# A mixer kernel on one core: nine r tiles beside attention, another order of the weight loads, and transposes on TensorE in both batches

## The chip, the cores and the metric

One core of a Trainium2 chip runs the kernel. Its engines are TensorE (PE, with the weight loads as PEld), VectorE (DVE), ScalarE (ACT), GpSimd (POOL) and SyncE (SP), which issues all DMAs here. The metric is the device time of one execution in microseconds, the median over several runs.

## The reference

Three blocks in a row, in float32, for 2 batches of 448 tokens and 768 channels:

```python
scores = scale * q @ k.T                       # 12 heads of 64, causal mask
x = softmax(scores) @ v                        # heads side by side: (2, 448, 768)
h = np.maximum(xt @ w_tok1, 0.0) @ w_tok2      # token mix, 448 -> 256 -> 448
u = x + h.transpose(0, 2, 1)
h2 = np.maximum(u @ w_ch1, 0.0) @ w_ch2        # channel mix, 768 -> 1536 -> 768
y = u + h2
# then a gated block: gelu(y @ w_in), layer norm of one half, a spatial 448 x 448
# product, the gate, w_out, and y added again
```

Most weights arrive as 8-byte floats and are decoded on the chip.

## The kernel before, in words

**Attention** (lines 251 to 558) goes over 24 heads, `n` = 0 to 23, batch 0 first, in pairs of heads (`pair`, line 400). Each head has two halves. For each half `probabilities` (line 327) multiplies q and k on PE (`s_ps`, line 345), masks and takes the maximum on DVE (line 350, tiles pe and mx), and exponentiates on ACT (line 359). The probabilities must then be transposed (tile pT). There are two ways. By DMA: ACT casts to a 16-bit high part (line 371), POOL subtracts for the low part (line 372, tile hl), SP issues a transposing DMA (line 373). On PE, with `on_pe`: four transposing matmuls into PSUM (line 365, t_ps), one eviction on ACT (line 367) and one on DVE (line 368). Only half (1, 1) of a pair can go on PE. `values` (line 386) multiplies by v (x_ps). After four heads `token_mix` (line 438) makes two channel tiles of u (a_ps, u_ps, tiles uh and ul).

**The channel mix** has twelve r tiles of 128 columns. One r tile for one batch is 18 matmuls of 448 columns (`mm3`, lines 185 to 187, r_ps), and needs one tile of w_ch1, which `load_w` (line 143) loads as 768 columns of 8 bytes (wraw, two buffers), decodes (`decode`, lines 127 to 131, on ACT and DVE), copies to a high part (line 140) and subtracts for the low part on POOL (`sub`, line 101, wlo). Three buffers hold decoded tiles.

The first NF0 = 8 r tiles of batch 0 are computed beside attention: `up_third` (line 495) emits a third of a tile, six matmuls, after each head of batch 1 from its fourth on, two after each of the last three; the rest follows as whole tiles (`up`, line 512). After attention the loop of line 633 computes batch 1 of the first eight tiles and both batches of the other four, loading those eight a second time. In between it asks for w_ch2 (`load_w2`, line 606) and scales r to 16 bits (`split_r`, line 594). Then come y = r times w_ch2 (y_ps, lines 671 to 696) and the gated block.

**What sets the order.** Each engine runs a fixed list. A scheduler makes the lists from a simulated timeline: of the instructions that are ready it takes the one of highest priority, which is the place in the program, moved by `tc.high_priority(offset=...)`; a negative offset moves it back. `tc.issue_after(ins)` keeps the block's instructions on the engine of `ins` behind it. `marks[n]` is the last transposing DMA issued up to head n; before, r tile m's load stands behind marks[10 + m].

Of the kernel before, what the change touches and what calls it, by code (L numbers as in the profile page):

```python
# [28 lines left out]
def mixer_kernel(  # L29
# [28 lines left out]
    GH = 4  # L58
    NT = T // P
    WC = 768  # L60
    NF0 = 8
    AHEAD = 4
    VAHEAD = 2
    LATER = 1500

    def f32(ap):
        return ap.bitcast(F32)
# [72 lines left out]
            nc.scalar.copy(hi, m)  # L140
        sub(lo, m, hi)

    def load_w(src, pool=wpool, bufs=3):

        k = src.shape[1]
        hi = pool.tile([P, WC // P, P], F32R, tag="whi", name="whi", bufs=bufs)[:, :k, :]
        lo = pool.tile([P, WC // P, P], F32R, tag="wlo", name="wlo", bufs=bufs)[:, :k, :]
        load64(hi.rearrange("p a f -> p (a f)"), lo.rearrange("p a f -> p (a f)"), src.rearrange("p a f -> p (a f)"))
        return hi, lo

    def absmax(dst, src):
# [65 lines left out]

    r_of = {}

    def channel_up(m, batches, pool, psum):  # L220

        wh, wl = load_w(w_ch1[m])
        for b in batches:
            us = slice(b * S, (b + 1) * S)
            pr = psum.tile([P, 512], F32, tag="d", name="r_ps")
            mm3(pr[:, :S], [((wh[:, c, :], wl[:, c, :]), (u_hi[c][b], u_lo[c][b])) for c in range(NCC)])
            r_done(m, b, pr, pool)
# [23 lines left out]
    with ExitStack() as at:  # L251
# [75 lines left out]
        def probabilities(qp, k2, hd, half, on_pe):  # L327

            ps = ps_s.tile([P, NP], F32, tag="s", name="s_ps")
            if (hd, half) == (1, 0):
                pe, mx = pes[count[0] % len(pes)], mxs[count[0] % len(pes)]
            else:
                pe = xp.tile([P, NP], F32, tag="pe", name="pe", bufs=NPE)
                mx = stp.tile([P, 2], F32, tag="mx", name="mx")
            todo, o = [], 0
            for j, i in enumerate(HALVES[half]):
                w = KW[i]
                if i > 0 or hd == 0:  # L340
# [13 lines left out]
            bias = mx  # L354
            if not on_pe:
                bias = stp.tile([P, 2], F32, tag="bias", name="bias")
                nc.scalar.add(bias, mx, math.log(PSCALE))
            for j, i, cs in todo:
                nc.scalar.activation(pe[:, cs], pe[:, cs], AF.Exp, bias=bias[:, j:j + 1], scale=-1.0)  # L359
            pT = hlp.tile([P, 2, NP // P, P], F16, tag="pT", name="pT", bufs=4)  # L360
            if on_pe:
                tp = ps_e.tile([P, 512], F32, tag="d", name="t_ps")
                for c in range(NP // P):
                    cs = slice(c * P, (c + 1) * P)
                    nc.tensor.matmul(tp[:, cs], pe[:, cs], ident, is_transpose=True, start=True, stop=True)
# [7 lines left out]
            last[0] = nc.sync.dma_start_transpose(  # L373
                out=pT.rearrange("p a c q -> p (a c) q"), in_=hl.rearrange("p a n -> p (a n)")
            ).ins
            return pT


# [59 lines left out]
        def token_mix(b, g, xf, xh, xl):  # L438
            N = GH * D
            pa = ps_a.tile([P, NT, N], F32, tag="a", name="a_ps")  # L440
            for t in range(NT):
                ts = slice(t * P, (t + 1) * P)
                nc.tensor.matmul(pa[:, t, :], w1h[:, 0, ts], xh[:, 0, :], start=True, stop=False)
                nc.tensor.matmul(pa[:, t, :], w1l[:, 0, ts], xh[:, 0, :], start=False, stop=False)
                mm3(pa[:, t, :], [((w1h[:, c, ts], w1l[:, c, ts]), (xh[:, c, :], xl[:, c - 1, :])) for c in range(1, NQ)], True)
            ah = xp.tile([P, NT, N], F32R, tag="ah", name="ah")
            al = xp.tile([P, NT, N], F32R, tag="al", name="al")
            nc.scalar.activation(ah, pa, AF.Relu)
# [22 lines left out]
                nc.vector.tensor_sub(u_lo[cc][b], pu[:, :S], f32(u_hi[cc][b]))  # L471


        last, last_x, marks = [None], [None], []
        order = [(b, h) for b in range(B) for h in range(H)]
        qks, vss = {}, {}

# [6 lines left out]
        def prepare_v(n):  # L484
            if n < len(order) and n % 2 == 0:
                b, h = order[n]

                with tc.high_priority(offset=-80):
                    vr, _ = v_begun.pop(n, None) or load_v(b, h // 2)
                    vss[b, h // 2] = prep_v(b, h // 2, vr)  # L490

        dense = list(range(NF0))
        thirds = []

        def up_third():

            if not thirds:
                m = dense.pop(0)
                with tc.issue_after(marks[H - 2 + m]), tc.high_priority(offset=-LATER):
                    wh, wl = load_w(w_ch1[m])  # L500
# [3 lines left out]
            mm3(  # L504
                pr[:, :S],
                [((wh[:, c, :], wl[:, c, :]), (u_hi[c][0], u_lo[c][0])) for c in (c0, c0 + 1)],
                c0 > 0, not thirds,
            )
            if not thirds:
                r_done(m, 0, pr, rpool)  # L510

        def up():

            m = dense.pop(0)
            with tc.issue_after(marks[H - 2 + m]):
                channel_up(m, [0], rpool, ps_e)

        def decode_tok(c):
            with tc.issue_after(last_mx[0]), tc.high_priority(offset=-80):
# [11 lines left out]
        for n, (b, h) in enumerate(order):  # L531
            if n > 0:
                prepare(n + AHEAD)
                prepare_v(n + VAHEAD)
            if n == GH - 1:
                for c in range(2, NQ):
                    load_tok(c)
                for c in range(NT):
                    load_tok2(c)
            if h % GH == 0:  # L540
                x = (
                    xp.tile([P, GH // 2, 7, D], F32, tag="xf", name="xf", bufs=2),
# [1 line left out]
                    xp.tile([P, NQ - 1, GH * D], F32R, tag="xl", name="xl"),  # L544
                )
            if h % 2 == 0:
                it = pair(b, h // 2, h % GH // 2, qks[b, h // 2], x, b == 0 and h > 0)
            next(it, None)
            marks.append(last[0])
            if h % GH == GH - 1:  # L550
                token_mix(b, h // GH, *x)

            if b == 1 and h >= 3:
                for _ in range(1 if h < H - 3 else 2):
                    up_third()

        while dense:
            up()
# [351 lines left out]
```

## Time and profile before

| | us |
|---|---|
| median of 3 runs | 415.42 (412.61 to 415.44) |
| profiled execution, its own time | 416.44 |
| its span, first to last instruction | 414.7 |
| PE busy | 391.3 (94%) |
| DVE, ACT, POOL busy | 282.4, 250.4, 202.5 |
| mean granted clock of TensorE | 0.988 of full speed |

The profile is of one execution. Busy times are sums over an engine's instructions; matmuls are pipelined, so PE counts as busy while one is under way. The DMA share is the mean busy share of 16 DMA engines; some stretches read above 1. Attention and the first r tiles fill the span to 168.8 us, the packed r stage goes to 228.3, the y stage to about 315, the gated block to the end.

### The profile page before, as it was taken

What the parts mean: (1) busy time and instruction counts of PE and PEld (TensorE: products, weight loads), DVE (VectorE), ACT (ScalarE), POOL (GpSimd) and SP (SyncE); (2) the same over time, 40 slices, a digit from 0 to 9 for tenths busy, and PEclk for the clock granted to TensorE, in tenths of its full rate; (3) what the DMA queues carried; (4) which work ended last, traced back from release to release, by engine and by line L of the source; (5) the groups of instructions that cost most, each with busy time, mean ns of one, the idle gap of its engine ahead of it and who ended that gap; (6) DMA issues with size and microseconds to landing.
All of it is one profiled execution on the core that took longest, in us unless ns stands there. A gap on an engine that the chain in (4) does not pass through costs nothing.

```text
span 414.7 us, 7332 instructions
## 1 busy us (share of the span) xinstructions
PE 391.3 (94%) x2622; PEld 267.9 (65%) x2622; DVE 282.4 (68%) x696; ACT 250.4 (60%) x483; POOL 202.5 (49%) x208
## 2 busy tenths in 40 slices
PE   5879899799898998999999999999999999999996
PEld 3447778588787887999889555555544445554554
DVE  6887866887785426444446787557898996469742
ACT  3988767787876555565679886344256556553210
POOL 3759864997686466062261447145121348315300
PEclk9999999799999999999999999999999999999999
DMA  7999899979997544466643313534623131100122
GB/s 220 246 238 232 161 206 271 246 186 236 265 247 140 137 112 144 163 217 229 207 149 102 90 65 114 186 107 134 222 73 90 51 103 51 52 2 0 68 92 107
DMA packets 61747, 61.77 MB, mean 149 GB/s; under 512 B 47888, under 2 KB 53264, under 8 KB 61712
## 3 DMA queue, kind: packets, MB, share of 16 engines
q1 hardware_dynamic: 61712, 61.32, 55.6%
q8 instruction: 20, 0.33, 0.3%
q14 instruction: 15, 0.12, 0.1%
HBM read 47.29 MB, written 2.75 MB: 121 GB/s over the span
## 4 chain that ended last, share of the span: by engine, by line
PE 25%; DVE 18%; ACT 12%; POOL 10%; DMA 9%; issue 8%; SPq 0%; POOLq 0%; ACTq 0%
DMA wraw<-in 7%; PE r_ps L186 5%; PE r_ps L185 5%; PE r_ps L187 5%; ACT r L172 3%; POOL hl L372 3%; PE o_ps L187 2%; PE o_ps L185 2%; PE o_ps L186 2%; DVE y L173 2%; DVE wm L131 2%; DVE w2m L131 1%; ACT wm L127 1%; PE u_ps L459 1%; POOL w L179 1%
## 5 line engine op out<-in xcount | busy, mean ns | idle before, releaser
L345 PE MATMUL s_ps<-k,q 128*128 128x64 f32 (+3 forms) x216 | 57.2, 405 | 11.5 <-DVE mx L350 4.8
L372 POOL TENSOR_TENSOR hl<-pe,hl 128x512 f16<-128x512 f32 x43 | 52.3, 1223 | 25.6 <-ACT hl L371 24.5
L101 POOL TENSOR_TENSOR wlo<-wm,whi 128x768 fp32r<-128x768 f32 x20 | 39.9, 1994 | 40.4 <-ACT whi L140 40.2
L185 PE MATMUL r_ps<-uh,whi 128*128 128x448 f32 x144 | 55.1, 383 | 0.0
L130 DVE TENSOR_SCALAR wm<-wm 128x768 int32<-128x768 int32 (+2 forms) x35 | 22.9, 655 | 46.9 <-ACT wm L127 46.9
L186 PE MATMUL r_ps<-ul,whi 128*128 128x448 f32 x144 | 53.9, 374 | 0.0
L187 PE MATMUL r_ps<-uh,wlo 128*128 128x448 f32 x144 | 53.0, 368 | 0.0
L185 PE MATMUL y_ps<-r,w 128*128 128x448 f16 x144 | 50.8, 353 | 0.0
L127 ACT ACTIVATE wm<-wraw 128x768 f32<-128x768 f32 (+2 forms) x35 | 27.8, 798 | 38.0 <-DMA wraw<-in 24.1
L186 PE MATMUL y_ps<-r,w 128*128 128x448 f16 x144 | 50.7, 352 | 0.0
L187 PE MATMUL y_ps<-r,w 128*128 128x448 f16 x144 | 50.6, 352 | 0.0
L345 PEld LDWEIGHTS s_ps<-k,q 128*128 128x128 f32 x216 | 32.2, 207 | 22.5 <-DVE mx L350 6.7
L350 DVE CUSTOM_DVE_ANT_0 pe<-s_ps,mask 128x192 f32<-128x192 f32 (+3 forms) x84 | 34.6, 441 | 7.2 <-PE s_ps L345 6.4
L246 POOL TENSOR_TENSOR y<-yt,ul 128x448 f32<-128x448 f32 x12 | 15.8, 1319 | 46.4 <-DVE yt L244 46.4
L359 ACT ACTIVATE pe<-pe,bias 128x448 f32<-128x448 f32 (+3 forms) x74 | 35.6, 525 | 0.4
L131 DVE SCALAR_TENSOR_TENSOR wm<-wraw,wm 128x768 int32<-128x768 int32 (+2 forms) x35 | 32.8, 938 | 0.7
L396 PE MATMUL x_ps<-vh,pT 128*128 128x65 f16 (+1 forms) x240 | 26.9, 201 | 3.1 <-DMA pT<-hl 3.0
L371 ACT CAST hl<-pe 128x512 f16<-128x512 f32 x43 | 26.3, 611 | 5.9 <-DMA pT<-hl 4.7
L185 PEld LDWEIGHTS r_ps<-uh,whi 128*128 128x128 f32 x144 | 27.3, 190 | 3.0 <-issue 0.4
L186 PEld LDWEIGHTS r_ps<-ul,whi 128*128 128x128 f32 x144 | 27.2, 189 | 3.1 <-issue 0.6
L187 PEld LDWEIGHTS r_ps<-uh,wlo 128*128 128x128 f32 x144 | 27.2, 189 | 2.7 <-issue 0.2
L179 POOL TENSOR_TENSOR w<-w2m,w 128x768 f16<-128x768 f32 x12 | 21.2, 1787 | 15.8 <-ACT w L178 11.2
(212 smaller groups left out, 1016.0 us busy)
## 6 DMA issues: line engine op xcount, KB each, us to landing
wraw<-in SPq DMA_DIRECT2D x36, 768.0 KB, 4.5
wraw<-in SPq DMA_DIRECT2D x14, 512.0 KB, 3.8
vr<-in SPq DMA_DIRECT2D x12, 320.0 KB, 4.0
k<-in SPq DMA_DIRECT2D x12, 224.0 KB, 3.7
q<-in SPq DMA_DIRECT2D x24, 112.0 KB, 4.0
out<-ob SPq DMA_DIRECT2D x11, 224.0 KB, 1.9
wraw<-in SPq DMA_DIRECT2D x3, 256.0 KB, 4.6
pT<-hl SPq DMA_TRANSPOSE x43, 4.0
```

The lines of the kernel that those rows point to most:

```text
L101: nc.gpsimd.tensor_sub(lo, src, f32(hi))
L127: nc.scalar.activation(m, words.bitcast(F32)[:, :, 1], AF.Prelu, scale=2.0 ** -112, alpha=-(2.0 ** 32))
L131: nc.vector.scalar_tensor_tensor(mi, words[:, :, 0], 29, mi, ALU.logical_shift_right, ALU.bitwise_or)
L185: nc.tensor.matmul(ps, lh, rh, start=i == 0 and not begun, stop=False)
L186: nc.tensor.matmul(ps, lh, rl, start=False, stop=False)
L187: done.append(nc.tensor.matmul(ps, ll, rh, start=False, stop=ended and i == n - 1).ins)
L345: last_s[0] = nc.tensor.matmul(ps[:, o:o + m], qp[:, q0:q0 + P], k2[:, ks], start=True, stop=True).ins
L350: last_mx[0] = nc.vector.tensor_tensor_reduce(out=pe[:, cs], in0=ps[:, cs], in1=mask0 if i == 0 else mask[:, MASKS[i]], scale=-1.0 / math. ...
L359: nc.scalar.activation(pe[:, cs], pe[:, cs], AF.Exp, bias=bias[:, j:j + 1], scale=-1.0)
L371: nc.scalar.copy(hl[:, 0], pe)
L372: nc.gpsimd.tensor_sub(hl[:, 1], pe, hl[:, 0])
L396: nc.tensor.matmul(o, ph, vh[:, c, h, :D + 1], start=j == 0, stop=False)
```

## The change

- NF0 becomes 9. Thirds are placed by a table of heads, from head 11 on, and their matmuls get a priority 150 lower. Four tiles still follow whole.
- The load of r tile m stands behind the transposes of head BEHIND[m]; the loads get a priority of -800 instead of -1500; the low part is subtracted in three parts of 256 columns.
- The half (1, 1) is transposed on PE for pairs 1, 2, 3 and 5 of batch 0 and 1, 2 and 3 of batch 1 (before: 1 to 5 of batch 0).
- The token weights are asked for at heads 2 and 3 instead of both at 3, the second with a priority raised by 100; v is prepared with -40 instead of -80.
- With NF0 the loop after attention runs over tiles 0 to 4, 9 to 11 and 5 to 8.

```diff
-    NF0 = 8
+    NF0 = 9
-    LATER = 1500
+    LATER = 800
+    BEHIND = [10, 15, 13, 13, 17, 18, 19, 12, 15]
+    THIRDS = {11: 1, 14: 1, 15: 1, 17: 1, 18: 2, 19: 1, 20: 1, 21: 3, 22: 2, 23: 2}
+    ON_PE = [(0, 1), (0, 2), (0, 3), (0, 5), (1, 1), (1, 2), (1, 3)]
...
+    def load_parts(src, behind):
+        raw = wpool.tile([P, WC], mybir.dt.int64, tag="wraw", name="wraw", bufs=2)
+        w = WC // len(behind)
+        for i, ins in enumerate(behind):
+            cs = slice(i * w, (i + 1) * w)
+            with tc.issue_after(ins):
+                nc.sync.dma_start(raw[:, cs], src[:, cs])
+        return raw
...
+        if behind is None:
+            load64(hi1, lo1, src)
+        else:
+            m = wpool.tile([P, WC], F32, tag="wm", name="wm", bufs=3)
+            decode(m, src, raw=load_parts(src, behind))
+            nc.scalar.copy(hi1, m)
+            w = WC // 3
+            for i in range(3):
+                cs = slice(i * w, (i + 1) * w)
+                sub(lo1[:, cs], m[:, cs], hi1[:, cs])
...
-                with tc.high_priority(offset=-80):
+                with tc.high_priority(offset=-40):
                     vr, _ = v_begun.pop(n, None) or load_v(b, h // 2)
...
+        def turns_from(n):
+            return [turns[min(marks[n] + i, len(turns) - 1)] for i in range(1)]
...
-                with tc.issue_after(marks[H - 2 + m]), tc.high_priority(offset=-LATER):
-                    wh, wl = load_w(w_ch1[m])
+                with tc.high_priority(offset=-LATER):
+                    wh, wl = load_w(w_ch1[m], behind=turns_from(BEHIND[m]))
...
+            with tc.high_priority(offset=-150):
+                mm3(
...
-            if n == GH - 1:
-                for c in range(2, NQ):
-                    load_tok(c)
-                for c in range(NT):
-                    load_tok2(c)
+            if n == 2:
+                with nullcontext():
+                    for c in range(2, NQ):
+                        load_tok(c)
+            if n == 3:
+                with tc.high_priority(offset=100):
+                    for c in range(NT):
+                        load_tok2(c)
...
-                it = pair(b, h // 2, h % GH // 2, qks[b, h // 2], x, b == 0 and h > 0)
+                it = pair(b, h // 2, h % GH // 2, qks[b, h // 2], x, (b, h // 2) in ON_PE)
...
-            if b == 1 and h >= 3:
-                for _ in range(1 if h < H - 3 else 2):
-                    up_third()
+            for _ in range(THIRDS.get(n, 0)):
+                up_third()
```

## Rows read from the trace of the kernel before

**Rows 1.** Busy time by stretch: PE, PEld, DVE, ACT, POOL, granted clock, DMA share, GB/s.
```profile
20.00:30.00 10.00, 7.83 (x58) 4.74 (x55) 8.44 (x32) 8.27 (x22) 5.13 (x7) 0.96 1.17 246
...
70.00:80.00 10.00, 7.65 (x64) 5.11 (x63) 7.63 (x24) 7.29 (x14) 8.00 (x9) 0.85 1.18 247
80.00:90.00 10.00, 10.00 (x94) 9.22 (x92) 8.62 (x24) 10.00 (x24) 9.66 (x9) 0.81 0.75 206
...
168.80:228.30 59.50, 59.50 (x294) 53.90 (x292) 30.62 (x53) 42.11 (x79) 22.23 (x11) 1.00 0.53 173
228.30:300.00 71.70, 71.70 (x385) 37.25 (x385) 52.38 (x101) 39.93 (x64) 30.26 (x19) 1.00 0.41 133
```

**Rows 2.** PE's timeline, 62 to 168.8: start, us, line, tiles, count, wait and releaser.
```profile
62.82 0.39 PE L186 MATMUL a_ps<-xl,w1h 128*128 128x256 f32 x1 [1.10 <-POOL xl L101]
...
75.75 1.02 PE L345 MATMUL s_ps<-k,q 128*128 128x448 f32 x2 [2.00 <-DVE mx L350]
...
109.51 0.20 PE L396 MATMUL x_ps<-vh,pT 128*128 128x65 f16 x1 [1.69 <-DMA pT<-hl]
...
133.39 0.20 PE L396 MATMUL x_ps<-vh,pT 128*128 128x65 f16 x1 [1.31 <-DMA pT<-hl]
...
161.22 0.39 PE L443 MATMUL a_ps<-xh,w1h 128*128 128x256 f32 x1 [0.68 <-POOL xh L101]
...
165.54 0.48 PE L459 MATMUL u_ps<-w2h,ah 128*128 128x448 f32 x1 [0.69 <-ACT ah L448]
```

**Rows 3.** SP's timeline of DMA issues in the first 80 us: start, us, line, tiles.
```profile
13.94 2.73 SPq L373 DMA_TRANSPOSE pT<-hl  x2
16.76 1.03 SPq L113 DMA_DIRECT2D wraw<-in  x2
...
25.29 0.93 SPq L113 DMA_DIRECT2D wraw<-in  x1
...
63.77 1.05 SPq L113 DMA_DIRECT2D wraw<-in  x2
...
67.08 5.50 SPq L373 DMA_TRANSPOSE pT<-hl  x2
...
73.38 0.47 SPq L113 DMA_DIRECT2D wraw<-in  x1
73.94 4.76 SPq L373 DMA_TRANSPOSE pT<-hl  x2
```

**Rows 4.** PE's timeline: four transposing matmuls, then the first and seventh of r matmuls.
```profile
36.69 0.60 PE L365 MATMUL t_ps<-ident,pe 128*128 128x128 f32 x4
...
199.69 0.37 PE L185 MATMUL r_ps<-uh,whi 128*128 128x448 f32 x1
...
200.92 0.37 PE L185 MATMUL r_ps<-uh,whi 128*128 128x448 f32 x1
```

**Rows 5.** Groups by line, shapes apart: count, busy us, mean ns, idle before, releasers.
```profile
L372 POOL TENSOR_TENSOR hl<-pe,hl 128x512 f16<-128x512 f32 x43 | 52.3, 1223 | 25.6 <-ACT hl L371 24.5 <-PE r_ps L186 0.8
L101 POOL TENSOR_TENSOR wlo<-wm,whi 128x768 fp32r<-128x768 f32 x20 | 39.9, 1994 | 40.4 <-ACT whi L140 40.2
...
L101 POOL TENSOR_TENSOR w1l<-wm,w1h 128x256 fp32r<-128x256 f32 x4 | 3.5, 886 | 0.2
L368 DVE SCALAR_TENSOR_TENSOR pT<-t_ps,pT 128x512 f16<-128x512 f32 x5 | 3.4, 674 | 0.0
...
L367 ACT ACTIVATE pT<-t_ps 128x512 f16<-128x512 f32 x5 | 2.9, 587 | 0.0
```

**Rows 6.** DMA queue, 138.9 to 149.5: packets, MB, share of 16 engines; issues, landing.
```profile
q1 hardware_dynamic: 2114, 0.52, 26.3%
...
pT<-hl SPq DMA_TRANSPOSE x3, 3.1
```

**Rows 7.** The same from 165.2 to 171, where one w_ch1 or w_ch2 load moves.
```profile
q1 hardware_dynamic: 144, 0.79, 43.5%
```

**Rows 8.** ACT's timeline near the end of the r stage: start, us, line, tiles.
```profile
221.79 6.83 ACT L172 ACTIVATE r<-r,rs 128x448 f16<-128x448 f32 x12
```

More of the change, by code (lines that the diff above doesn't have):

```diff
@@ L141, in load64, with load_w @@
         sub(lo, m, hi)
-    def load_w(src, pool=wpool, bufs=3):
+    def load_parts(src, behind):
[6 more added lines that the diff above has]
+        return raw
+    def load_w(src, pool=wpool, bufs=3, behind=None):
         k = src.shape[1]
@@ L147, in load_w @@
         lo = pool.tile([P, WC // P, P], F32R, tag="wlo", name="wlo", bufs=bufs)[:, :k, :]
-        load64(hi.rearrange("p a f -> p (a f)"), lo.rearrange("p a f -> p (a f)"), src.rearrange("p a f -> p (a f)"))
+        src, hi1, lo1 = (t.rearrange("p a f -> p (a f)") for t in (src, hi, lo))
+        if behind is None:
[8 more added lines that the diff above has]
+                sub(lo1[:, cs], m[:, cs], hi1[:, cs])
         return hi, lo
@@ L218, in mixer_kernel, with channel_up @@
     r_of = {}
-    def channel_up(m, batches, pool, psum):
-        wh, wl = load_w(w_ch1[m])
+    def channel_up(m, batches, pool, psum, behind=None):
+        wh, wl = load_w(w_ch1[m], behind=behind)
         for b in batches:
@@ L372, in probabilities @@
             nc.gpsimd.tensor_sub(hl[:, 1], pe, hl[:, 0])
-            last[0] = nc.sync.dma_start_transpose(
+            turns.append(nc.sync.dma_start_transpose(
                 out=pT.rearrange("p a c q -> p (a c) q"), in_=hl.rearrange("p a n -> p (a n)")
-            ).ins
+            ).ins)
             return pT
@@ L444, in token_mix @@
                 nc.tensor.matmul(pa[:, t, :], w1l[:, 0, ts], xh[:, 0, :], start=False, stop=False)
-                mm3(pa[:, t, :], [((w1h[:, c, ts], w1l[:, c, ts]), (xh[:, c, :], xl[:, c - 1, :])) for c in range(1, NQ)], True)
+                amm = mm3(pa[:, t, :], [((w1h[:, c, ts], w1l[:, c, ts]), (xh[:, c, :], xl[:, c - 1, :])) for c in range(1, NQ)], True)
+            last_a[0] = amm[-1]
             ah = xp.tile([P, NT, N], F32R, tag="ah", name="ah")
@@ L471, in token_mix @@
                 nc.vector.tensor_sub(u_lo[cc][b], pu[:, :S], f32(u_hi[cc][b]))
-        last, last_x, marks = [None], [None], []
+        turns, last_x, last_a, marks = [], [None], [None], []
         order = [(b, h) for b in range(B) for h in range(H)]
@@ L498, in up_third @@
                 m = dense.pop(0)
-                with tc.issue_after(marks[H - 2 + m]), tc.high_priority(offset=-LATER):
-                    wh, wl = load_w(w_ch1[m])
+                with tc.high_priority(offset=-LATER):
+                    wh, wl = load_w(w_ch1[m], behind=turns_from(BEHIND[m]))
                 pr = ps_e.tile([P, 512], F32, tag="d", name="r_ps")
@@ L503, in up_third, with up @@
             m, pr, wh, wl, c0 = thirds.pop(0)
[L504 to L508, printed above, removed]
+            with tc.high_priority(offset=-150):
+                mm3(
+                    pr[:, :S],
+                    [((wh[:, c, :], wl[:, c, :]), (u_hi[c][0], u_lo[c][0])) for c in (c0, c0 + 1)],
+                    c0 > 0, not thirds,
+                )
             if not thirds:
                 r_done(m, 0, pr, rpool)
-        def up():
+        def up(behind=None):
             m = dense.pop(0)
-            with tc.issue_after(marks[H - 2 + m]):
-                channel_up(m, [0], rpool, ps_e)
+            with tc.issue_after(behind) if behind else nullcontext():
+                channel_up(m, [0], rpool, ps_e, turns_from(BEHIND[m]))
         def decode_tok(c):
@@ L546, in mixer_kernel @@
             if h % 2 == 0:
-                it = pair(b, h // 2, h % GH // 2, qks[b, h // 2], x, b == 0 and h > 0)
+                it = pair(b, h // 2, h % GH // 2, qks[b, h // 2], x, (b, h // 2) in ON_PE)
             next(it, None)
-            marks.append(last[0])
+            marks.append(len(turns) - 1)
             if h % GH == GH - 1:
                 token_mix(b, h // GH, *x)
-            if b == 1 and h >= 3:
-                for _ in range(1 if h < H - 3 else 2):
-                    up_third()
+            for _ in range(THIRDS.get(n, 0)):
+                up_third()
         while dense:
```

## The prediction

> **What bounds the kernel now.** I read the busy time by stretch first. From 168.8 us on TensorE (PE) has no idle time: 59.50 of 59.50 us in the r stage and 71.70 of 71.70 in the y stage [rows 1]. There time is the number of matmuls times their cadence. Before 168.8 the picture is another: in 70 to 80 PE is busy 7.65 of 10 us while the DMA share is 1.18, and the granted clock is 0.85 there and 0.81 in 80 to 90 [rows 1]. [...] 20 to 30 has a smaller dip (0.96) and a DMA share of 1.17.
>
> Then PE's own timeline, for who ended its waits [rows 2]. Between 62 and 168.8 us six are longer than half a microsecond: 1.10 us for POOL's xl, 2.00 for DVE's mx at 75.75 (the clock falls right behind it), 1.69 and 1.31 for pT, the DMA transposes, at 109.51 and 133.39, and 0.68 and 0.69 around the last token mix: 7.47 us. Everything else is either PE at work or matmuls too closely spaced for the view to show a gap.
>
> Then SP's queue, because transposes and weight loads share it [rows 3]. At 13.94 two transposes take 2.73 us to issue. At 67.08, right behind two w_ch1 loads at 63.77, two take 5.50, and at 73.94, right behind another load, 4.76. So weight loads in the first quarter of batch 1 hold up the transposes that attention waits for.
>
> The rule for the sum: time is PE's work plus PE's waits. An r matmul that moves into attention gains only if it falls into a wait.
>
> **The change, part by part.** The dictionary THIRDS adds up to 15 thirds (1+1+1+1+2+1+1+3+2+2), not the seventeen of the title, against 12 before (six heads with one, three with two). So five r tiles are in thirds, four follow whole as before, nine in all.
>
> *The ninth tile.* Six r matmuls take 1.23 us (199.69 to 200.92) [rows 4], a tile of 18 takes 3.7. The packed stage loses one tile, attention gains one. That is -3.7 and +3.7: nothing by itself, and at most 3.7 as filler for waits, which I count where the waits stand.
>
> *PE transposes.* Five pairs before (1 to 5 of batch 0), seven after: pair 4 of batch 0 leaves, pairs 1, 2, 3 of batch 1 come. Net two halves more. PE: four transposes take 0.60 us [rows 4], two halves 1.2 us. DVE gets 0.674 each; ACT swaps a cast for an eviction of 0.587; POOL loses 1.223 each [rows 5]. These three are below 9 of 10 us busy in most stretches of batch 1, so I put nothing there. PE's 1.2 is paid in full: **+1.2**; the lower bound is 0.5, eight matmuls at 128/448 of the r cadence of 0.205.
>
> In batch 1 three of 24 transposes leave SP and the DMA queues. Three transposes took 26.3% of a 10.6 us stretch, but the landing of the third is outside it: about 2.8 us for 0.52 MB, that is two, 1.4 us of all engines each [rows 6]. So 4.2 us of DMA time go from batch 1. The two waits for pT are 3.0 us; the halves that PE transposes no longer wait at all, the others have a shorter queue, and a third at low priority may run in what is left. Bounds 0 and -3.0; I take **-2.5**, near the rows, since their releaser is named.
>
> [...]
>
> *The weight loads.* Before, four were tied to heads 10 to 13; two went out at 63.77, one at 73.38 [rows 3], the fourth behind them. After, tile 0 alone stays behind head 10; tile 1 waits for head 15's transposes, and since wraw has two buffers and thirds ask in order, tiles 2 and 3 come with it or later. Two to three loads of 2.5 us [rows 7] leave the stretch of 64 to 80, whose second half has a DMA share of 1.18 [rows 1]. If the mx wait of 2.00 at 75.75 goes, the dip behind it (3.4 us) may go too. Bounds 0 and -5.4. The releaser of that wait is DVE, not a DMA, so the DMA is only one step behind it; I take a little over half, **-3.0**. What is late next there: ACT, at 10.00 of 10 in 80 to 90 [rows 1].
>
> [...]
>
> *The split subtraction.* POOL's wlo takes 1.994 us for 768 columns, and 0.886 for 256 (w1l) [rows 5]. Three parts are 2.66 us: +0.66 on POOL for each of nine tiles, 6 us spread over 80, on an engine that idles half of the span. In exchange hl, xl and xh stand behind at most 0.9 us. Bounds -0.7 and +0.7, taken as 0.
>
> *The ninth load.* One more tile is loaded and decoded for batch 0 and again for batch 1: 2.5 us DMA, 2.66 POOL and its share of ACT and DVE. It lies beside attention. Bounds 0 and +2 (ACT full in 80 to 90); taken as 0.
>
> *Token weights and v.* The four loads of token weights had gone out by 25.29 us, two at 16.76 [rows 3]; asking for them a head earlier can pull them by some microseconds, into a stretch with a DMA share of 1.17. The v preparation moves by 40 steps. Nothing shows a wait for w1 or w2, so no gain; the cost is bounded by the two 512 KB loads, 1.7 us each at 0.31 MB per us plus issue, 4.4 us at most. Taken as 0.
>
> *After attention.* The load of the first w2 tile stands behind r tile 9 instead of 8, and the r stage is 3.7 us shorter. split_r's ACT run begins at 221.79 [rows 8], 6.5 us before the y stage that needs its first piece, and it moves with the r stage. 0, at worst +1.
>
> Sum against the profiled execution's own 416.44 us (span 414.7 and 1.8 around it): 416.4 + 1.2 - 2.5 - 3.0 = 412.1. The median of the runs shown is 415.42, 1.0 lower, so the forecast is **411.1 us**, 1.0% faster. One per cent is about what a measurement of this kernel tells from no change, and the forecast lies on that edge.
>
> **The rivals.**
> (a) All named waits and the dip go: 1.2 - 3.0 - 5.4 gives 409.2, less 1.0: **408.2**. For it: every one of these waits is DMA-near, and low-priority thirds from head 11 on can fill them. Against: PE's order is fixed beforehand, so filler stands in front of or behind a late wait, not in it. With the xl wait (1.1), the end's 1.4 and the lower bounds of the transposes (0.7) and of the split (0.7) as well it would be 404.3.
> (b) The waits move. More matmuls stand between attention's own, ACT and DVE end at the same time, and the 1.2 us of transposes is added: **416.6**. For it: ACT 10.00 and PE 10.00 of 10 in 80 to 90. Against: both pT waits are for a queue that gets shorter.
> (c) Slower: the early token loads. Two 512 KB loads go ahead of q, k and the transposes of heads 2 to 5, where DMA is full and PE has no r tile to fill with. It decides from about 3 us of delay on; at 4.4 with nothing gained, 415.4 + 1.2 + 4.4 = **421.0**. For it: share 1.17 at 20 to 30. Against: the loads were already early.
> That the change does not do what its title says is true of the count; two further thirds would move 2.5 us from one side of 168.8 to the other and leave the sum as it is.
>
> **How the numbers follow.** Forecast 0.45 (its own range 408.5 to 413.5), (a) 0.16, (b) 0.21, (c) 0.18. Faster by over 1% (below 411.3): (a) and 0.28 of the forecast, 0.44. Within 1%: the rest of the forecast and most of (b), 0.36. Slower by over 1% (above 419.6): (c) and a little of (b), 0.20. The range 404.3 to 419.5 reaches from (a) with all lower bounds to (b) with the upper ones of the ninth load (2) and the y stage (1); most of (c) is left out.
>
> **What would show it.** Right: r begins its packed run with 270 matmuls instead of 288; granted clock 1.00 in 70 to 90; no PE wait over 1 us for pT in batch 1; SP's transposes behind 64 us at under 1.5 us of issue each; the last a_ps no later than 161 us though 15 thirds lie before. Wrong: a new wait of PE in the first 60 us (c); the last token mix later than 165 us with the same idle sum (b); r matmuls of the packed stage with gaps, which would say that nine tiles' weights come too slowly.

## The result and the profile after

The change made the kernel slower: 418.95 us, median of 4 runs (416.74 to 422.14), against 414.68 beside it, a ratio of 1.0105 (95% interval 1.0064 to 1.0147). The forecast was 411.1, faster by 1%; the range reached to 419.5. The profiled execution is the fastest of the four, 416.74 us with a span of 415.0, so its trace shows the change at its best. The execution profiled before, 416.44 us, is 1.0 above the median beside it, so the two spans, 414.7 and 415.0, hide most of the loss. In a second measurement the ratio was 1.0089 (first experiment).

Busy time by stretch after the change, with the columns of [rows 1]; the last line is the whole time up to the first packed r matmul:

```profile
20.00:30.00 10.00, 7.73 (x61) 4.72 (x57) 9.12 (x34) 9.06 (x22) 6.31 (x7) 1.00 1.18 269
70.00:80.00 10.00, 7.47 (x88) 5.40 (x86) 4.97 (x14) 7.32 (x17) 5.55 (x12) 1.00 1.03 197
80.00:90.00 10.00, 10.00 (x68) 8.39 (x67) 6.48 (x25) 7.98 (x17) 6.91 (x7) 1.00 0.55 112
...
180.00:228.30 48.30, 48.30 (x239) 43.14 (x238) 27.72 (x44) 35.02 (x66) 20.32 (x10) 1.00 0.54 175
228.30:300.00 71.70, 71.25 (x382) 36.85 (x380) 52.48 (x102) 40.04 (x64) 30.21 (x19) 1.00 0.40 133
...
0.00:171.18 171.18, 150.82 (x1391) 121.14 (x1391) 118.50 (x346) 122.09 (x266) 119.20 (x157) 1.00 0.85 204
```

The stretch that the forecast looked at did what it was to do: the DMA share in 70 to 80 fell from 1.18 to 1.03, the granted clock there rose from 0.85 to 1.00 and in 80 to 90 from 0.81 to 1.00, and ACT at 80 to 90 fell from 10.00 to 7.98. (The second profile of the kernel before, below, has a clock of 1.00 there too.) Yet PE is busy only 7.47 of 10 us in 70 to 80, no more than before (7.65). The last line gives the sum: 171.18 less 150.82 of PE's work are 20.36 us without work ahead of the packed r stage. The same view of the kernel before gave 168.77 less 150.02, that is 18.75, and 20.7 in its second profile (below; up to there PE was busy 150.02 us at a mean granted clock of 0.97 in the first and 147.99 at 0.99 in the second, for the same work, so idle time reads shorter in the first). With a ninth tile to fill with, PE waited no less.

PE's timeline after the change (start, us, line, tiles, count, wait and releaser, as in [rows 2]):

```profile
62.28 0.39 PE L209 MATMUL a_ps<-xl,w1h 128*128 128x256 f32 x1 [0.75 <-POOL xl L104]
...
76.09 0.20 PE L419 MATMUL x_ps<-vh,pT 128*128 128x65 f16 x1 [0.58 <-DMA pT<-hl]
...
78.94 1.24 PE L368 MATMUL s_ps<-k,q 128*128 128x64 f32 x4 [1.16 <-DVE mx L373]
...
97.71 1.98 PE L368 MATMUL s_ps<-k,q 128*128 128x128 f32 x8 [1.02 <-DVE mx L373]
...
129.81 0.39 PE L466 MATMUL a_ps<-xh,w1h 128*128 128x256 f32 x1 [1.97 <-POOL xh L104]
...
168.73 0.47 PE L483 MATMUL u_ps<-w2h,al 128*128 128x448 f32 x1 [1.07 <-DVE al L473]
...
171.18 0.45 PE L208 MATMUL r_ps<-uh,whi 128*128 128x448 f32 x1
...
227.01 0.36 PE L208 MATMUL y_ps<-r,w 128*128 128x448 f16 x1
```

The two waits for pT over 1 us are gone, as forecast, and the mx wait of 2.00 is two of 1.16 and 1.02. In their place stands one of 1.97 for POOL's xh, in front of a token mix; before, no wait for xh was longer than 0.68. The r stage begins 2.4 us later (168.77 before); it is shorter by one tile, so the y stage begins 1.3 us earlier (228.3 before).

SP's queue of DMA issues after the change, as in [rows 3]:

```profile
64.40 0.58 SPq L153 DMA_DIRECT2D wraw<-in  x1
65.56 8.61 SPq L396 DMA_TRANSPOSE pT<-hl  x4
...
87.68 0.58 SPq L153 DMA_DIRECT2D wraw<-in  x1
88.78 0.42 SPq L153 DMA_DIRECT2D wraw<-in  x1
...
91.32 6.68 SPq L396 DMA_TRANSPOSE pT<-hl  x3
```

One load of w_ch1 is left before 80 us where there were four; the second goes out at 87.68. The four transposes behind it take 8.61 us to issue, 2.2 each, where two took 5.50 and 4.76, 2.8 and 2.4 each. That is faster, but not the under 1.5 us that the prediction named as a sign of being right. How much the loads do to them is seen where they are put back, below.

ACT's timeline near the end of the r stage, as in [rows 8], and PE's waits by releaser from 225 us to the end (total, times, longest):

```profile
221.99 6.81 ACT L195 ACTIVATE r<-r,rs 128x448 f16<-128x448 f32 x12
```

```profile
PE gt_ps L188 <- DVE gtam L181: 1.7, 1, 1.7
PE ys_ps L188 <- DVE yam L181: 0.6, 1, 0.6
PE y_ps L210 <- POOL w L202: 0.5, 1, 0.5
```

split_r starts at 221.99 as it did at 221.79, though the y stage that needs it comes 1.3 us earlier: the lead is 5.0 us instead of 6.5. From the first y matmul to the end the changed kernel takes 188.0 us (415.0 less 227.0), the one before 186.4 (414.7 less 228.3). In these two profiles, what the shorter r stage gave, the y stage and the gated block took.

### The profile page after: what moved, and what is told of

The parts are those of the page before. It is cut to its first block, busy times and chain, and to the rows that moved or that the text cites. A ratio compares the mean times of both kernels' runs of the same rounds, so it can differ in the third digit from the quotient of the medians.

```text
span 415.0 us, 7364 instructions
## 1 busy us (share of the span) xinstructions
PE 388.6 (94%) x2630; PEld 265.0 (64%) x2630; DVE 284.7 (69%) x700; ACT 252.8 (61%) x483; POOL 206.3 (50%) x225
## 4 chain that ended last, share of the span: by engine, by line
DVE 23%; DMA 22%; PE 17%; ACT 14%; POOL 12%; issue 10%; SPq 1%; ACTq 0%; POOLq 0%; DVEq 0%
DMA wraw<-in 19%; DVE wm L134 3%; ACT r L195 3%; ACT wm L130 3%; DVE w2m L134 2%; PE s_ps L368 2%; POOL hl L395 2%; PE o_ps L209 2%; PE o_ps L210 2%; PE o_ps L208 2%; DVE wm L133 2%; DVE y L196 2%; DVE pe L373 2%; DMA pT<-hl 2%; POOL w L202 2%
## 5 line engine op out<-in xcount | busy, mean ns | idle before, releaser
L368 PE MATMUL s_ps<-k,q 128*128 128x64 f32 (+3 forms) x216 | 54.4, 392 | 12.0 <-DVE mx L373 6.5
L104 POOL TENSOR_TENSOR wlo<-wm,whi 128x256 fp32r<-128x256 f32 (+1 forms) x39 | 45.0, 1179 | 39.4 <-ACT whi L143 31.6
L395 POOL TENSOR_TENSOR hl<-pe,hl 128x512 f16<-128x512 f32 x41 | 51.2, 1257 | 23.6 <-ACT hl L394 21.5
L133 DVE TENSOR_SCALAR wm<-wm 128x768 int32<-128x768 int32 (+2 forms) x36 | 25.2, 700 | 44.7 <-ACT wm L130 44.7
L130 ACT ACTIVATE wm<-wraw 128x768 f32<-128x768 f32 (+2 forms) x36 | 28.8, 803 | 42.1 <-DMA wraw<-in 26.8
L209 PE MATMUL r_ps<-ul,whi 128*128 128x448 f32 x144 | 53.0, 371 | 0.0
L210 PE MATMUL r_ps<-uh,wlo 128*128 128x448 f32 x144 | 52.6, 367 | 0.0
L208 PE MATMUL y_ps<-r,w 128*128 128x448 f16 x144 | 50.8, 352 | 0.0
L209 PE MATMUL y_ps<-r,w 128*128 128x448 f16 x144 | 50.8, 352 | 0.0
L368 PEld LDWEIGHTS s_ps<-k,q 128*128 128x128 f32 x216 | 30.7, 199 | 22.4 <-DVE mx L373 7.5
L382 ACT ACTIVATE pe<-pe,bias 128x448 f32<-128x448 f32 (+3 forms) x70 | 33.7, 528 | 0.5
L394 ACT CAST hl<-pe 128x512 f16<-128x512 f32 x41 | 25.0, 613 | 6.2 <-DMA pT<-hl 5.9
L419 PE MATMUL x_ps<-vh,pT 128*128 128x65 f16 (+1 forms) x240 | 25.3, 197 | 1.7 <-DMA pT<-hl 1.4
```

Source lines behind the costliest of these rows:

```text
L104: nc.gpsimd.tensor_sub(lo, src, f32(hi))
L130: nc.scalar.activation(m, words.bitcast(F32)[:, :, 1], AF.Prelu, scale=2.0 ** -112, alpha=-(2.0 ** 32))
L133: nc.vector.tensor_scalar(mi, mi, 3, None, ALU.logical_shift_left)
L208: nc.tensor.matmul(ps, lh, rh, start=i == 0 and not begun, stop=False)
L209: nc.tensor.matmul(ps, lh, rl, start=False, stop=False)
L210: done.append(nc.tensor.matmul(ps, ll, rh, start=False, stop=ended and i == n - 1).ins)
```

## The experiments

All ratios are to the kernel before on the same chip. "r at" is the start of the packed r stage, "idle" PE's time without work up to there (from the busy time by stretch), "y at" the first y matmul, "lead" y less the start of split_r. Each is of one profiled execution.

| run | us | ratio (95%) | r at | idle | y at | lead |
|---|---|---|---|---|---|---|
| before, twice | 414.95 (second) | 1.001 (0.998 to 1.0041) | 168.8, 168.7 | 18.8, 20.7 | 228.3, 228.2 | 6.5, 6.9 |
| changed, twice | 419.19 (second) | 1.0089 (1.0058 to 1.012) | 171.2, 174.2 | 20.4, 21.8 | 227.0, 230.1 | 5.0, 5.9 |
| changed, loads back | 416.24 | 1.0028 (0.9994 to 1.0061) | 169.9 | 17.9 | 225.8 | 3.5 |
| changed, pairs back | 416.58 | 1.0035 (1.0006 to 1.0065) | 169.6 | 18.8 | 225.5 | 2.7 |
| changed, eight tiles | 416.75 | 1.003 (0.9992 to 1.0069) | 168.9 | 19.9 | 228.4 | 5.2 |
| changed, token loads back | 421.99 | 1.0174 (1.0129 to 1.0219) | 174.4 | 20.8 | 230.2 | 3.8 |
| before + transposes | 413.74 | 0.9954 (0.9925 to 0.9983) | 165.8 | 16.8 | 225.3 | 6.2 |
| the same again | 413.59 | 0.9983 (0.9953 to 1.0012) | 166.5 | 19.6 | 226.1 | 6.9 |
| before + nine tiles | 415.59 | 1.0012 (0.9982 to 1.0042) | 170.7 | 19.5 | 226.5 | 4.5 |
| before + loads, split | 419.74 | 1.0107 (1.0057 to 1.0157) | 172.6 | 22.2 | 232.2 | 6.9 |
| before + loads, unsplit | 423.06 | 1.0168 (1.013 to 1.0205) | 175.8 | 24.1 | 235.4 | 6.6 |

**Both kernels again.** No edit.

> The changed kernel once more, to see how far its executions lie apart and what a second profile shows. If its loss is in the order of its instructions, about 419 us again, ratio 1.005 to 1.015, and waits of PE for POOL and DVE in batch 1 at the same places. If it is in the clock, the granted clock of the slow executions is lower than 0.99 and explains 3 us or more of them.

> The kernel before once more, for a second profile. If the 5 us of half-speed clock in its first profile were an accident of that execution, this one has a mean granted clock of 0.994 or more, and its packed r stage starts 1.5 to 5 us earlier than 168.8. If the dip belongs to the order of the instructions, the clock falls at 77 us again and the stage starts at 168 to 169. Ratio 1.000 within its interval in both.

The loss repeated: 419.19 us and 1.0089. In this execution of the changed kernel the wait for xh stood at the same instruction, 1.97 us again, at 131.56, and its stretches (columns as above) show what came behind it:

```profile
130.00:132.00 2.00, 0.44 (x3) 0.41 (x3) 1.33 (x3) 2.00 (x6) 1.76 (x4) 1.00 0.98 347
132.00:138.00 6.00, 5.73 (x67) 5.45 (x65) 2.31 (x3) 3.07 (x6) 5.24 (x6) 0.72 0.45 142
```

PE worked 0.44 of 2 us, then the granted clock was 0.72 for six. The kernel before, in its second profile:

```profile
70.00:80.00 10.00, 8.10 (x99) 5.74 (x97) 7.91 (x25) 7.57 (x16) 8.26 (x9) 1.00 1.08 262
80.00:90.00 10.00, 9.77 (x85) 8.48 (x86) 8.75 (x23) 10.00 (x23) 9.62 (x10) 1.00 0.83 217
```

The dip of [rows 1] is absent here, the list of instructions is the same, and the r stage begins at the same time (168.7). The dip was of one execution. Without it the r stage begins no earlier, so its 3.4 us were not there to be gained.

**One part of the change undone.** Four kernels, each the changed one with one part as before.

```diff
-                with tc.high_priority(offset=-LATER):
-                    wh, wl = load_w(w_ch1[m], behind=turns_from(BEHIND[m]))
+                with tc.issue_after(turns[marks[min(H - 2 + m, len(marks) - 1)]]), tc.high_priority(offset=-LATER):
+                    wh, wl = load_w(w_ch1[m])
...
-    LATER = 800
+    LATER = 1500
```

> The change with the r tiles' loads as before: behind heads 10, 11, 12 and so on, priority -1500, the low part in one subtraction. If late weights or the split subtraction in POOL's queue are the cause, the time falls to 415 or less, and the waits for POOL's xh and xl shrink from 4.7 us to under 3. If not, 418 to 420, and the lower clock behind 77 us, seen before the change, is back.

```diff
-    ON_PE = [(0, 1), (0, 2), (0, 3), (0, 5), (1, 1), (1, 2), (1, 3)]
+    ON_PE = [(0, 1), (0, 2), (0, 3), (0, 4), (0, 5)]
```

> The change with the transposes on PE for pairs 1 to 5 of batch 0 as before. If PE's transposes in batch 1 cost what was gained (ACT and DVE evictions in front of the next head's maximum), the time falls to 415 or less, ratio below 1.002. If they help, by fewer transposing DMAs, it rises to 420 or more. If the ninth tile is the cause, 418 to 420 again.

```diff
-    NF0 = 9
+    NF0 = 8
-    THIRDS = {11: 1, 14: 1, 15: 1, 17: 1, 18: 2, 19: 1, 20: 1, 21: 3, 22: 2, 23: 2}
+    THIRDS = {15: 1, 16: 1, 17: 1, 18: 1, 19: 1, 20: 1, 21: 2, 22: 2, 23: 2}
```

> The change with eight r tiles and the thirds of before, all else kept. If the ninth tile is what delays attention (its 3.7 us stand in front of late attention matmuls), the packed r stage starts 3 to 4 us earlier than in the changed kernel, with 288 matmuls, and the time falls to about 415, ratio 0.998 to 1.004. If loads or transposes are the cause, it stays at 418 to 420, ratio above 1.006.

```diff
-            if n == 2:
-                with nullcontext():
-                    for c in range(2, NQ):
-                        load_tok(c)
-            if n == 3:
-                with tc.high_priority(offset=100):
-                    for c in range(NT):
-                        load_tok2(c)
+            if n == GH - 1:
+                for c in range(2, NQ):
+                    load_tok(c)
+                for c in range(NT):
+                    load_tok2(c)
...
-                with tc.high_priority(offset=-40):
+                with tc.high_priority(offset=-80):
```

> The change with token weights and the preparation of v as before. If the earlier token loads slow batch 0 (rival c of the prediction): 415 or less, ratio below 1.002, first token mix not later than in the changed kernel. If they are without effect, as the unchanged start of the changed profile says (first a_ps at 45 us in both): 418 to 420, ratio above 1.006.

Three of the four take back 2.4 to 3.0 us of 419.19, each by itself, so they cannot be added up, and none comes down to the 415 of the kernel before. With the loads back the stretch up to the r stage reads:

```profile
0.00:169.90 169.90, 151.98 (x1390) 122.83 (x1391) 115.59 (x344) 120.20 (x266) 114.02 (x139) 0.99 0.85 203
```

169.90 less 151.98 is 17.9 us idle, the lowest of the kernels with nine tiles, against 20.4 and 21.8 with the new loads.

SP's queue and PE's timeline of this kernel, with two loads ahead of the transposes as before the change:

```profile
65.14 12.01 SPq L396 DMA_TRANSPOSE pT<-hl  x4
```

```profile
76.03 0.27 PE L419 MATMUL x_ps<-vh,pT 128*64 128x65 f16 x2 [3.74 <-DMA pT<-hl]
```

Behind one load the same four transposes took 8.61 us, and no wait of PE for pT was longer than 0.58. So the loads did hold up the transposes, as the prediction read it, and moving them did gain here. What the changed kernel has instead is the wait of 1.97 us for xh at 129.81, which the kernel with the loads back does not have. Ahead of it, ACT and then POOL of the changed kernel:

```profile
120.96 0.91 ACT L130 ACTIVATE wm<-wraw 128x768 f32<-128x768 f32 x1 [1.19 <-DMA wraw<-in]
121.78 0.60 ACT L394 CAST hl<-pe 128x512 f16<-128x512 f32 x1
```

```profile
122.51 1.97 POOL L395 TENSOR_TENSOR hl<-pe,hl 128x512 f16<-128x512 f32 x1 [1.51 <-DVE wm L133]
```

ACT waits 1.19 us for a weight tile that has not arrived, and the cast of hl, which attention needs, stands behind it. POOL idles 1.51 us before it can subtract for hl. (The profile names DVE's pass over the weight tile as what ended this; the cast ended within 0.1 us of it.) From there POOL works without a gap until xh is done at 129.75, and its next subtraction of weights comes only at 130.79. So a late load reaches the token mix here through ACT's queue. In the second profile of the changed kernel ACT waits 1.32 us at the same place. Between 110 and 130 us it waits 3.6 and 4.0 us for weight tiles in the two profiles of the changed kernel, 0.9 and 1.0 in those of the kernel before, and not at all with the loads back. The kernels with eight tiles and with the old pairs do not have the wait for xh at this place (theirs are 3.25 us for pT at 121.67, and 1.35 for xh at 159.05), so it takes the parts together.

The fourth kernel, with the token loads as before, went the other way: it is at 421.99. Rival (c) falls: in this company the early token loads help.

**One part alone.** The kernel before with the new set of pairs, with nine tiles and the table of thirds, and with the loads' new places, priority and split (then without the split, and the split by itself). The set of pairs was timed twice.

```diff
-                it = pair(b, h // 2, h % GH // 2, qks[b, h // 2], x, b == 0 and h > 0)
+                it = pair(b, h // 2, h % GH // 2, qks[b, h // 2], x, (b, h // 2) in ON_PE)
```

> The kernel before with the new set of pairs transposed on PE alone. If the transposes in batch 1 cost attention what they save in DMA: 415 to 418, ratio 1.001 to 1.007, and the packed r stage starts 1 to 3 us later than in the kernel before (168.8). If they help: ratio below 0.998 and no wait for pT over 1 us.

> The kernel before with the new transposes alone, once more. If its gain is real: ratio 0.993 to 0.998, packed r stage from 164 to 167 us, no wait for pT over 1 us behind 100 us. If it was chance of four executions: 0.998 to 1.002.

```diff
-    NF0 = 8
+    NF0 = 9
...
-            if b == 1 and h >= 3:
-                for _ in range(1 if h < H - 3 else 2):
-                    up_third()
+            for _ in range(THIRDS.get(n, 0)):
+                up_third()
```

> The kernel before with nine r tiles and the new table of thirds alone; loads, priorities, transposes and token weights as before. If attention absorbs nothing of the ninth tile and the load line gives back what the r stage saves: 415 to 418, ratio 1.000 to 1.006, packed r stage 3 to 5 us later than in the kernel before. If the ninth tile is good and the other edits spoil it: 411 to 413, ratio below 0.996.

```diff
-                with tc.issue_after(marks[H - 2 + m]), tc.high_priority(offset=-LATER):
-                    wh, wl = load_w(w_ch1[m])
+                with tc.high_priority(offset=-LATER):
+                    wh, wl = load_w(w_ch1[m], behind=turns_from(BEHIND[m]))
```

> The kernel before with the new places of the w_ch1 loads, their priority and the split subtraction alone; eight tiles, thirds as before. If the new load order is bad by itself: 416 to 419, ratio 1.003 to 1.010, split_r later than 222.5. If it only hurts together with the ninth tile: ratio 0.997 to 1.003.

```diff
-            w = WC // 3
-            for i in range(3):
-                cs = slice(i * w, (i + 1) * w)
-                sub(lo1[:, cs], m[:, cs], hi1[:, cs])
+            sub(lo1, m, hi1)
```

> The kernel before with the new places of the w_ch1 loads and their priority, the subtraction in one part. If the places are the price (the second load leaves at 88 us instead of 64, and all later ones are later by 5 to 10 us): 418 to 420, ratio 1.006 to 1.014, packed r stage from 170 us or later. If the split was the price: 0.997 to 1.003.

> The kernel before with the low part of the loads beside attention subtracted in three parts, nothing else. If the extra 0.66 us of POOL per tile is the price of the new loads: ratio 1.005 to 1.012. If the split is free: 0.997 to 1.003.

The transposes alone have the lowest time of all: 0.9954 and 0.9983, an r stage that begins 2.2 to 3.0 us earlier. The second interval reaches to 1.0012, so a gain of some 1 to 2 us is likely and not certain. PE's waits for pT between 62 us and the r stage (total, times, longest), in the kernel before and with the transposes:

```profile
PE x_ps L396 <- DMA pT<-hl: 3.0, 2, 1.7
...
PE x_ps L397 <- DMA pT<-hl: 3.7, 3, 2.8
```

In the second profiles of the two they are 5.3 and 5.0. So these waits did not fall; they came together at 76 us, 2.79 and 3.50 us long. What fell are the waits for mx, from 2.3 and 1.7 us to 0.4 and 0.2, and those for POOL's xl and xh, from 2.3 and 2.5 to 0.5 and 1.1.

Nine tiles alone are worth nothing, 1.0012: the r stage begins 1.9 us later, the y stage 1.8 earlier, and the lead of split_r falls from 6.5 to 4.5. A third that was to fill waits makes one there itself, 2.52 us for its wlo at 76.25.

The loads' places (with their priority) alone lose 1.68%, and here most of the loss can be read. The chain of work that ended last, of the kernel with the new places unsplit, before the last token mix (start, us, what):

```profile
153.12 2.54 POOL wlo L104
155.66 0.02 issue
155.69 0.90 ACT wm L130
156.58 0.73 ACT whi L143
157.31 0.07 issue
157.38 2.52 POOL wlo L104
159.90 0.02 issue
...
161.62 2.46 POOL wlo L104
164.08 0.22 POOL xh L455
...
165.07 0.69 POOL xh L104
```

Three decodes run one behind the other, POOL's subtraction of 2.5 us and ACT's pass over the next tile in turn, and xh, which the token mix waits for, stands behind the third in POOL's queue. PE's timeline and the stretches of the same kernel show the price:

```profile
165.82 0.58 PE L463 MATMUL a_ps<-xh,w1h 128*128 128x256 f32 x1 [3.97 <-POOL xh L104]
```

```profile
160.00:166.00 6.00, 2.03 (x11) 1.53 (x10) 3.23 (x7) 4.48 (x8) 4.07 (x6) 0.98 0.66 238
166.00:170.00 4.00, 3.34 (x14) 3.04 (x15) 0.58 (x1) 0.25 (x2) 3.21 (x2) 0.50 0.56 184
```

PE works 2.03 of 6 us, and then stand four us at a granted clock of 0.50, by which some 2 us more were lost (an estimate, half of the four). Only one load goes out before 80 us instead of four (63.01, then two at 87.21), and the decoding runs one tile later: by 153 us POOL has begun seven subtractions of w_ch1, against eight in the kernel before. Three waits for pT, 2.22, 1.13 and 1.65 us between 86 and 106, stand beside this.

With the split the loss is 1.07%; there the waits are 2.16 and 2.08 us for pT at 87 and 105, and 3.20 us for xh at 137.88. The intervals of the two overlap, and two of the three subtractions in the chain above are of tiles loaded a second time, which the split leaves whole. So that the split helps here is not shown. On the old places the split alone does nothing good (1.0026, 1.0001 to 1.005). The loads' places and their priority were not tried apart, nor the lower priority of the thirds by itself.

**The line of loads after attention.** The kernel before with one unused load and decode more; the changed kernel with one load less (the last early tile's second batch uses the weights of the tile before it, so one weight tile is neither loaded nor decoded); and the changed kernel with its last early tile's second batch moved to the front, where its weights are still there.

```diff
+            if m == NF0:
+                spare = load_w(w_ch1[m])
             channel_up(m, [1] if m < NF0 else [0, 1], r1pool, ps_d)
```

> The kernel before with one tile of w_ch1 loaded and decoded once more in the packed r stage and not used. Theory of the load line (load, ACT, DVE, POOL with two raw buffers sets when the y stage gets its weights, and the change adds a load to it): split_r's run on ACT starts 3 to 4 us later than before, y waits, and the time rises by 2 to 4 us, ratio 1.004 to 1.010. If only TensorE counts there: ratio 0.999 to 1.003, split_r within 1 us of the r stage's own shift.

```diff
-        wh, wl = load_w(w_ch1[m], behind=behind)
+        if m == NF0 - 1 and batches == [1]:
+            wh, wl = last_w[0]
+        else:
+            wh, wl = last_w[0] = load_w(w_ch1[m], behind=behind)
```

> The change without the last load of w_ch1 in the r stage: tile 8's second batch is computed with the weights of the tile before it, so one load and its decoding are left out and the output of that tile is another. Load line theory: split_r starts 3 to 4 us earlier than in the changed kernel, the waits in the y stage go, 1.5 to 4 us less than the changed kernel, ratio 1.000 to 1.006. If the load line is not what gives back: 419, ratio 1.007 or more.

```diff
-for m in [*range(NF0 - tail), *range(NF0, NFF), *range(NF0 - tail, NF0)]:
+for m in [NF0 - 1, *range(NF0 - tail), *range(NF0, NFF), *range(NF0 - tail, NF0 - 1)]:
```

> The change, where the last r tile beside attention keeps its decoded weights and its second batch comes first after attention: one load of w_ch1 less. Load line theory: split_r starts 3 us earlier, the waits in the y stage (1.5 us in the changed kernel) go, 1.5 to 3 us less than the changed kernel, ratio 1.001 to 1.006 against before. If the loss is all in attention: 419 again, ratio 1.007 or more.

The unused load cost 1.46% (420.31, 1.0085 to 1.0207). split_r moved from 221.3 to 225.86, though PE has no more to do (its ACT timeline, then its PE waits by releaser):

```profile
225.86 5.70 ACT L172 ACTIVATE r<-r,rs 128x448 f16<-128x448 f32 x10
```

```profile
PE y_ps L187 <- POOL w L179: 1.4, 1, 1.4
...
PE r_ps L187 <- POOL wlo L101: 1.0, 1, 1.0
```

With one load less the changed kernel is at 417.26 (1.0049, 1.0019 to 1.0078); split_r began at 221.2, which is 48.2 us after the start of the r stage instead of 50.8 and 50.0, and the lead was 7.6. So behind attention the loads and their decoding move split_r. That a gain comes from there is not shown: the interval overlaps that of the changed kernel, and from the first y matmul to the end this kernel takes 187.2 us, as the changed one did in its second profile (187.1). The third run missed: one load less, but 422.92 us. Its order brings r tile 11 one group later, split_r begins at 226.0, and the rest of the kernel takes 193.1 us from the first y matmul. It changed two things, and says nothing on the load.

**Two parts together.** The transposes with the nine tiles, with the token and v edits, and with the split.

> The kernel before with the new transposes and with nine tiles and the table of thirds; loads and priorities as before. If the two add: 0.9954 times 1.0012, about 413.5 to 414.5, ratio 0.994 to 0.999. If the load line takes back what attention gains: the r stage begins before 168, split_r stays at 219 to 222 us, its lead over the y stage shrinks to under 4 us, waits in the y stage appear, ratio 0.997 to 1.003.

> The kernel before with the new transposes and the earlier token weights and v, which helped inside the change (422.0 without them). If they help by themselves: 410 to 412.5, ratio 0.988 to 0.994, first a_ps before 45.5 us. If their effect there was only another order of all that follows: 0.994 to 1.000, packed r stage as in the kernel with the transposes alone (165.8).

> The new transposes with the subtraction in three parts beside attention. The split shortens what stands in POOL's queue ahead of xh and xl: if that adds, 0.990 to 0.995. If only the order of the instructions changes by it: 0.995 to 1.003.

416.36 (1.0031, 1.0004 to 1.0057), 417.73 (1.0069, 1.0042 to 1.0096) and 421.33 (1.015, 1.0102 to 1.0199). The ninth tile takes back what the transposes gained: r stage at 170.9, lead 4.4. The token edits, without which the changed kernel is 2.8 us slower, cost this one some 4; and the split, free by itself, costs nearly 8 with the transposes. The trace of the last one has a wait of 3.83 us for xh at 163.21 behind two whole subtractions, the same place as above, though here the loads stand where they stood: later loads are not the only way to it. Its mean clock was 0.983, and I take only the place from it.

## Why the prediction was wrong

**The weight loads, -3.0: the step that failed, and in its sign.** The prediction priced what the loads do where they stood and put nothing on what they do where they land. Where they stood it was right in kind: undone in the changed kernel, they slow four transposes from 8.61 to 12.01 us, and the longest wait for pT is 3.74 us instead of 0.58. But undone they also give back 3.0 us in all (419.19 to 416.24), and alone they cost 1.7%, with the split 1.1%. In the changed kernel ACT waits for a late weight tile, and xh comes 1.97 us late to the second token mix of batch 1; with the new places alone POOL's subtractions stand ahead of xh, and the last token mix waits 3.97. [Rows 2] showed the place of the last, two waits of 0.68 and 0.69 around it. The split, priced at 0.66 us a tile, is cheaper; the profile's group by line after the change, mixing the 256-column parts with the whole subtractions of other stages:

```profile
L104 POOL TENSOR_TENSOR wlo<-wm,whi 128x256 fp32r<-128x256 f32 (+1 forms) x39 | 45.0, 1179 | 39.4 <-ACT whi L143 31.6
```

In the timeline three parts take 2.13 us, 0.14 more than the 1.994 of [rows 5], not 0.66. Its zero was right on the old places (1.0026 alone); on the new ones the kernel with it is 0.6% lower, with intervals that overlap.

**The clock dip.** Of the 5.4 us from which the -3.0 was taken, 3.4 were an estimate of what one execution lost at granted clocks of 0.85 and 0.81 in two stretches of ten us, 1.5 and 1.9 [rows 1]; in that trace the clock is 0.50 in each us from 77 to 83 and 0.61 in the next. No run shows the 3.4 us as a gain: with 1.00 in both stretches the second profile has the r stage at 168.7. Over 28 executions of the kernel before, the mean granted clock was 0.9945 (0.987 to 1.000), from which I estimate a mean loss of 0.55% or 2.3 us, where the profiled one had lost 1.2% at 0.988; over seven of the changed kernel it was 0.9934. So some 2.3 us were the most to gain, and nothing of it was gained.

**Waits for pT, -2.5, and PE's transposes, +1.2: near in number, by luck.** By themselves these edits gave -1.9 and -0.7 us where -1.3 stood. But the waits for pT were 3.7 and 5.0 us with them and 3.0 and 5.3 without: the time came out of the waits for mx, which the prediction had laid to the loads, and for xl and xh, which it had left out. Why those fell is not shown. In the changed kernel, with the loads moved too, the two waits over 1 us went and the sum for pT is 1.4 and 1.6 us; in its time the gain is not to be seen.

**The ninth tile, nothing by itself: right** (1.0012 alone). Beside the other edits it is not nothing: 2.4 us in the changed kernel, 2.6 with the transposes. That thirds would fill waits did not come true: idle time is 19.5 us with the tile alone and 20.4 and 21.8 in the change, against 18.8 and 20.7. This was the prediction's own sign for rival (b), a last token mix later than 165 us with the same idle sum (a u_ps of it waits at 168.73; before, at 165.54). By its number rival (c), 421.0, came closest (2.05 us off, (b) at 416.6 is 2.35 off), but by luck, since its cause fell. The *ninth load* was counted twice in the prediction, beside attention and again for batch 1. It is one in all: 21 tiles are decoded instead of 20, twelve of them behind attention in both kernels.

**After attention, 0: wrong in part.** The step said that split_r's run "moves with the r stage". It followed only part of the way: with 18 r matmuls fewer behind attention (3.7 us) it began 2.2 us sooner after the start of the r stage (50.8 us instead of 53.0 in the first profiles, 50.0 instead of 52.6 in the second; 52.4 and 53.1 with loads or pairs back). Its twelve weight tiles have fewer matmuls to be decoded beside, and the runs with one load more and one less moved it by 4 us and 1 to 3 us. From the first y matmul to the end of the span the changed kernel takes 188.0 and 187.1 us, against 186.4 before (186.9 with nine tiles alone, 188.7 with pairs back). How much of that the shorter lead costs is open: two kernels with eight tiles and a lead of 6.9 us, the split alone and the loads with the split, take 187.7 too.

**Token weights, 0 (to +4.4).** The 0.31 MB per us under the 4.4 is 0.79 MB in 43.5% of 5.8 us [rows 7]. Rival (c) fell in the changed kernel; the changed kernel is 2.8 us slower with the old places than with the new. Why the same edit costs some 4 us with the transposes alone is open. Any one of these edits gives PE, ACT and POOL other lists from end to end, and the parts don't add up: the sum of what they cost alone or in pairs isn't the cost of the change. What can be said of the change as a whole is where its time went: PE's idle time ahead of the r stage did not fall, its work there rose by the tile and the transposes, and the shorter r stage was partly given back behind it.

The version with the lowest time is the kernel before with the new set of pairs alone, 413.6 to 413.7 us against 415.0; that it is faster is likely, not certain.

## What to carry to other kernels

When loads are moved out of a crowded stretch, find the queue of each engine that decodes them at their new place, and name what stands behind them there; here a weight tile ahead of what TensorE waits for cost more than the slow transfers had, and the loads put back gave 3.0 us in all. Read whether work that is moved as filler lowers the sum of idle time; here it was 20.4 and 21.8 us against 18.8 and 20.7. Read too whether the loads of a stage made shorter by it come earlier by as much; here split_r came 2.2 us sooner after the start of an r stage with 3.7 us less work. A dip of the clock seen in one profile isn't a gain in store: look at a second execution of the same kernel first, which here had 1.00 where the first had 0.85.

## What was not expected of the hardware

Executions of one and the same list differ in the granted clock, 0.987 to 1.000 over 28 of them, which by an estimate from these two figures is some 5 us of 415. Their times do not follow it alone: the three at 1.000 took 413.15, 413.36 and 415.75 us, and the slowest, 419.03, had 0.996. Two profiles at 0.988 and 0.995, by the same estimate 5.0 and 2.1 us lost, have the r stage begin at 168.8 and 168.7 all the same: the difference came out of idle time (18.8 against 20.7). Three deep falls followed idle stretches: 0.50 from 77 us in the first profile of the kernel before, where PE worked 0.24 of 2 us from 74 to 76; 0.50 in the four us behind 2.03 of 6 us of work; 0.72 in the six behind 0.44 of 2. But the changed kernel's first profile has the same 1.97 us wait, with 0.19 of 2 us of work from 128 to 130, and a clock of 1.00 from 130 to 138, so one such wait decides nothing by itself.

The time that SP took to issue transposing DMAs went with the loads ahead of them. At 65 us, four took 8.61 us behind one load of w_ch1 in the changed kernel, and 7.04 (3.70 and 3.34) in the kernel before with the loads' new places alone. Behind two they took 12.01 in the changed kernel with the loads back, and 10.26 and 9.25 in the two profiles of the kernel before, with a third load between the first two transposes and the last two.
